# Clustered attention and a softplus feed-forward: the first batch prepared by head pairs, split weights for half of the first pass, and matmuls without data in TensorE's waits

## The chip, the cores and the metric

The kernel runs on 1 core of a Trainium2 chip. The metric is the device time of one execution in microseconds (us). A core has TensorE (PE, matmuls and transposes by matmul into PSUM), VectorE (DVE), ScalarE (ACT), GpSimd (POOL) and SyncE (SP, which here issues DMA transposes and stores). Each engine works through its own rows in order; semaphores order them against each other.

## The reference

Attention over 4 batches of 8 heads, 768 tokens, 64 channels, in which a query sees only the keys of its own cluster; then a feed-forward layer with softplus:

```python
q_n = q / (norm(q) + 1e-06); k_n = ...; c_n = ...           # unit vectors
q_assign = argmax(einsum('bhsd,hcd->bhsc', q_n, c_n))       # 16 clusters a head
k_assign = argmax(einsum('bhsd,hcd->bhsc', k_n, c_n))
mask = q_assign[..., :, None] == k_assign[..., None, :]
scores = where(mask, q @ k.T / sqrt(D), -1e9)
attn = exp(scores - max); attn = attn / (sum(attn) + 1e-9)
x = (attn @ v)                                              # 3072 tokens x 512
h = x @ w_in                                                # 512 x 2048
out = (max(h, 0) + log1p(exp(-abs(h)))) @ w_out             # 2048 x 512
```

Inputs are float32, the two weight matrices float64. The kernel keeps float32 accuracy with pairs of float16 numbers (a high part and the rest).

## The kernel before, in words

The work goes in eight passes: four batches, each in two halves of the queries. A pass has 24 score tiles (8 heads, 3 tiles of 128 queries each). A tile's steps are: `scores`, four matmuls on TensorE against all 768 keys (L544; the second half of the contraction holds the low parts and 16 columns that carry the mask); the row maximum on VectorE (L560); the exponential on ScalarE (L568); then the attention weights must be turned so that keys lie on partitions. In the first pass this is done in float32: six transposes on TensorE (L585), one half evicted by ScalarE (L593), the other by VectorE (L591), and `attend` multiplies in float32 (L647). In the other passes the weights are split (ScalarE casts the high part, L607, GpSimd subtracts, L609), and two tiles together go through one DMA transpose of 24 blocks, a *flip*, issued by SP (L209); `attend` then takes 18 short float16 matmuls (L651 to L653). After two heads the output is normalised (VectorE L670 to L678), split (L685, L687) and turned by a flip of 6 blocks into `xT`.

Before a batch's scores, `prep_k` (two heads at a time) and `prep_q` (four heads) split the inputs, turn them (on TensorE for batch 0, by flips later) and find each token's cluster: short matmuls against the centroids (L394, L395) and some nine VectorE rows on them. `clusters` marks the clusters that hold a key.

The feed-forward part of a pass is `ffn1` (16 blocks of 12 matmuls, `softplus` behind each) and `ffn2` (two halves, three tiles, 24 matmuls each). It starts when all four `xT` pieces of its pass are there and runs beside the scores of the next pass. `prep_weights` splits the float64 weights in 32 steps of 512 columns: a load, one row on ScalarE, three on VectorE (L305, L309, L315), a cast on ScalarE (L318), a subtraction on GpSimd (L319).

What sets the order: the class `Order` runs all these as coroutines while the program is built. Each step names its engine and a cost; the planner takes the step that can start soonest by these costs, the lower priority number first, and emits its instruction. So each engine's order is fixed at build time. Rings (`ring("h", 2)` and the like) stand for the buffers.

## Time and profile before

| | us |
|---|---|
| median of 3 runs | 906.73 (905.98 to 908.38) |
| profiled execution | 904.0 |
| its span | 902.2 |
| TensorE busy | 823.7 (91%) |
| ScalarE busy | 589.4 (65%) |
| VectorE busy | 560.8 (62%) |
| GpSimd busy | 523.9 (58%) |
| mean granted TensorE clock | 0.973 |

The span runs from the first to the last instruction of the profiled execution. An engine's share is an average over the whole span; the views by stretch of time, which the prediction shows, tell the stages apart. "PEclk" is the clock that TensorE was granted.

### The profile page before, as it was taken

To read this page: it belongs to the slowest core of one execution; us is meant where nothing else is said; L and a number is where in the kernel's file an instruction comes from. 1 tells how busy PE (TensorE), PEld (TensorE's weight loads), DVE (VectorE), ACT (ScalarE), POOL (GpSimd) and SP (SyncE) were. 2 spreads that over 40 slices of the span, in tenths; PEclk is the share of its full clock that TensorE was granted. 3 is DMA by queue.
4 is the path that set the end of the run, shared out by engine and by line. 5 is a ranking of instruction groups with operands and counts; after the bars stand their busy time and mean duration, and the time that the engine had idled before them with its cause. 6 is when DMAs were issued, how large, how long until landed. Compare 5 with 4: busy or idle time off the path is not lost.

```text
span 902.2 us, 19238 instructions
## 1 busy us (share of the span) xinstructions
PE 823.7 (91%) x7843; PEld 520.0 (58%) x7843; DVE 560.8 (62%) x1034; ACT 589.4 (65%) x904; POOL 523.9 (58%) x353
## 2 busy tenths in 40 slices
PE   2669797889679999999999999999999999999996
PEld 2558684555335666666666666666666666655542
DVE  5889787778685665675766666666665645433331
ACT  5657477886458877876767777867677676633320
POOL 5233326896548778777677676776676565512210
PEclk9979699999799999999999999999999999999998
DMA  6323439999546979999888779998867755600000
GB/s 222 95 94 120 130 128 195 199 226 237 141 123 159 202 171 202 223 203 230 157 199 179 162 149 206 207 211 182 171 155 161 133 115 138 126 9 25 12 1 35
DMA packets 393320, 136.02 MB, mean 151 GB/s; under 512 B 369680, under 2 KB 386064, under 8 KB 393232
## 3 DMA queue, kind: packets, MB, share of 16 engines
q1 hardware_dynamic: 371472, 99.15, 54.9%
q10 hardware_dynamic: 21760, 35.66, 13.0%
q8 instruction: 61, 1.00, 0.5%
q14 instruction: 27, 0.22, 0.1%
HBM read 35.68 MB, written 6.29 MB: 47 GB/s over the span
## 4 chain that ended last, share of the span: by engine, by line
PE 72%; DMA 4%; DVE 3%; POOL 3%; issue 2%; ACT 2%; POOLq 0%; DVEq 0%; ACTq 0%
PE s L544 10%; PE o L786 9%; PE o L784 9%; PE o L785 9%; PE h L720 8%; PE h L722 8%; PE h L721 8%; PE av L651 3%; PE av L653 3%; PE av L652 3%; DMA pt<-phl 3%; POOL phl L609 2%; DMA xT<-xn 1%; ACT p L568 1%; DVE negm L560 1%
## 5 line engine op out<-in xcount | busy, mean ns | idle before, releaser
L609 POOL TENSOR_TENSOR phl<-p,phl 128x768 f16<-128x768 f32 x168 | 277.2, 1666 | 90.9 <-ACT phl L607 54.2
L560 DVE TENSOR_REDUCE negm<-s 128x1 f32<-128x768 f32 x192 | 182.9, 954 | 67.5 <-PE s L544 65.2
L568 ACT ACTIVATE p<-s,negm 128x768 f32<-128x768 f32 x192 | 172.3, 898 | 72.9 <-DVE negm L560 47.7
L763 POOL TENSOR_TENSOR gh<-fg,gh 128x768 f16<-128x768 f32 x64 | 105.7, 1652 | 134.5 <-ACT gh L762 134.0
L720 PE MATMUL h<-xT,wi 128*128 128x384 f16 x512 | 167.9, 328 | 14.6 <-DVE fg L751 6.2
L722 PE MATMUL h<-xT,wi 128*128 128x384 f16 x512 | 168.1, 328 | 0.0
L721 PE MATMUL h<-xT,wi 128*128 128x384 f16 x512 | 168.0, 328 | 0.0
L544 PE MATMUL s<-kt,qt 128*128 128x384 f16 x768 | 158.5, 330 | 10.2 <-ACT p L568 10.0
L784 PE MATMUL o<-wo,gh 128*128 128x512 f16 x384 | 146.3, 381 | 4.9 <-ACT gh L762 3.3
L786 PE MATMUL o<-wo,gh 128*128 128x512 f16 x384 | 146.5, 382 | 1.4 <-POOL gh L763 1.4
L785 PE MATMUL o<-wo,gh 128*128 128x512 f16 x384 | 146.4, 381 | 0.1
L741 ACT ACTIVATE fa<-fa 128x384 f32<-128x384 f32 x128 | 66.6, 521 | 114.8 <-DVE fa L739 114.1
L607 ACT CAST phl<-p 128x768 f16<-128x768 f32 x168 | 134.1, 827 | 7.1 <-DMA pt<-phl 5.5
L739 DVE TENSOR_SCALAR fa<-h 128x384 int32<-128x384 int32 x128 | 71.1, 556 | 104.0 <-PE h L722 102.8
L651 PE MATMUL av<-vb,pt 128*128 128x65 f16 x1008 | 108.7, 192 | 1.9 <-DMA pt<-phl 1.8
L652 PE MATMUL av<-vb,pt 128*128 128x64 f16 x1008 | 108.7, 192 | 0.0
L653 PE MATMUL av<-vb,pt 128*128 128x65 f16 x1008 | 108.4, 194 | 0.0
L544 PEld LDWEIGHTS <-qt 128*128 128x128 f16 x768 | 72.7, 99 | 58.5 <-issue 15.1
L751 DVE SCALAR_TENSOR_TENSOR fg<-h,fa 128x384 f32<-128x384 f32 x128 | 70.6, 552 | 57.1 <-ACT fa L742 54.5
L651 PEld LDWEIGHTS <-pt 128*128 128x128 f16 x1008 | 93.6, 98 | 15.7 <-DMA pt<-phl 3.4
L652 PEld LDWEIGHTS <-pt 128*128 128x128 f16 x1008 | 92.9, 97 | 11.8
L653 PEld LDWEIGHTS <-pt 128*128 128x128 f16 x1008 | 93.1, 97 | 0.0
(114 smaller groups left out, 1193.6 us busy)
## 6 DMA issues: line engine op xcount, KB each, us to landing
wo<-in_moe_w_in_dram ACTq DMA_DIRECT2D x16, 512.0 KB, 3.6
wo<-in_moe_w_out_dram ACTq DMA_DIRECT2D x14, 512.0 KB, 3.9
rawk<-in_k_dram ACTq DMA_DIRECT2D x16, 384.0 KB, 4.8
rawv<-in_v_dram ACTq DMA_DIRECT2D x16, 384.0 KB, 4.8
rawq<-in_q_dram ACTq DMA_DIRECT2D x16, 384.0 KB, 4.2
out_dram<-ot SPq DMA_DIRECT2D x24, 256.0 KB, 2.5
pt<-phl SPq DMA_TRANSPOSE x84, 5.5
wraw<-in_moe_w_out_dram ACTq DMA_DIRECT2D x2, 512.0 KB, 3.7
```

The costliest lines, as they stand in the source:

```text
L544: nc.tensor.matmul(st[:, j, :SH], qt[:, s, i], kt[:, s, NT // 2 * j : NT // 2 * (j + 1)], start=(s == 0), stop=(s == 1),)
L560: yield op("DVE", 950, lambda: nc.vector.tensor_reduce(negm, st[:, :, :SH], AX.XY, ALU.max, negate=True))
L609: "POOL", 1640, lambda: nc.gpsimd.tensor_tensor(phl[:, u, 1], p32, phl[:, u, 0], ALU.subtract), shared=True
L651: nc.tensor.matmul(av, pt[:, 0, c], vb[:, c, D : 2 * D + 1], start=(c == 0), stop=False)
L652: nc.tensor.matmul(av[:, :D], pt[:, 0, c], vb[:, c, :D], start=False, stop=False)
L653: nc.tensor.matmul(av, pt[:, 1, c], vb[:, c, D : 2 * D + 1], start=False, stop=(c == NT - 1))
L720: nc.tensor.matmul(hp, w[0], x[0], start=(c == 0), stop=False)
L721: nc.tensor.matmul(hp, w[0], x[1], start=False, stop=False)
L722: nc.tensor.matmul(hp, w[1], x[0], start=False, stop=(c == NP - 1))
L784: nc.tensor.matmul(po, g[0], wo[:, f, 0, 0], start=(f == f0), stop=False)
L785: nc.tensor.matmul(po, g[0], wo[:, f, 0, 1], start=False, stop=False)
L786: nc.tensor.matmul(po, g[1], wo[:, f, 0, 0], start=False, stop=(f == f0 + NF // 2 - 1))
```

## The change

The planner and the start of the program change; the arithmetic of each step stays, except where it says so.

- **Head pairs.** Batch 0's Q is prepared two heads at a time (`first_q`), a score tile waits for its own two heads, K's two layouts share one buffer, and the low-part copy on ScalarE goes for batch 0. Early results may use whichever PSUM bank is free (`bank`); evictions go to the engine that the planner finds free (`evict`).
- **Split weights from tile 12 on.** `MIX` has one letter for two tiles: the first six pairs of the first pass stay float32, the other six take the split path with flips.
- **Fill-ins.** Before a TensorE step with a planned wait over 600 ns, `warm` emits matmuls of 120 columns on constants into an unused part of the attention bank, as many as fill 65% of the wait at 52 ns each: 1251 in the program.
- **Weight steps in pace.** Step s waits for score tile 1.4 s.
- **The last `xT` piece** of the first pass is turned by TensorE; the planner's DMA model has separate clocks for loads and flips, and a subtraction or cast may be given to VectorE at a penalty of 2000 ns, which the new order never does.

```diff
+WGATE = 0
+WPACE = 1.4
+WARM = 120
+WARM_FROM = 600
+WARM_SHARE = 0.65
+MIX = "ffffffhhhhhh"
+EARLY = "hos"
+PTB = "ho"
...
             self.active.remove(ch)
-            _, eng, ns, emit, opt = ch["op"]
+            if eng == "PE" and self.warm:
+                self.warm(start - self.free["PE"])
...
+    mbank = ps_m.tile([P, 512], F32, name="mbank")
+    idle = mbank[:, 512 - WARM :]
+
+    def warm(gap):
+
+        if gap > WARM_FROM:
+            for _ in range(int(gap * WARM_SHARE / 52)):
+                nc.tensor.matmul(idle, eye, ones[:, :WARM], start=True, stop=True)
...
+    def evict(dst, src, size):
+
+        return op(
+            ("ACT", "DVE"),
+            (180 + size * 0.8, 160 + size * 1.04),
+            (lambda: nc.scalar.copy(dst, src), lambda: nc.vector.tensor_copy(dst, src)),
+        )
+
+    def sub(dst, a, b, size):
+
+        return op(
+            ("POOL", "DVE"),
+            (150 + size * 1.95, 120 + size * 1.08),
+            [lambda e=e: e.tensor_tensor(dst, a, b, ALU.subtract) for e in (nc.gpsimd, nc.vector)],
+            shared=True,
+            bias=BIAS,
+        )
+
+    banks = {"s": (ps_s, 2), "h": (ps_h, 2), "o": (ps_o, 1)}
+
+    def bank(tags, shape, dtype, name):
+
+        tag = next((t for t in tags if od.room(t, banks[t][1])), tags[0])
+        key = yield from ring(tag, banks[tag][1])
+        return key, banks[tag][0].tile(shape, dtype, tag=tag, name=name)
...
-        yield op("ACT", 630, lambda: nc.scalar.activation(mag, val, AF.Abs, scale=sc))
+        gate = int(WGATE + step * WPACE)
+        if gate >= 0:
+            yield wait("sc", gate)
+        yield op("ACT", 660, lambda: nc.scalar.activation(mag, val, AF.Abs, scale=sc))
...
-        yield op("ACT", 830, lambda: nc.scalar.copy(n2[:, :, :D], n1[:, :, D:]))
-        od.set(nk)
+        if n >= H:
+            k2, n2 = yield from next_n2()
+            keys.append(k2)
+            yield op("ACT", 830, lambda: nc.scalar.copy(n2[:, :, :D], n1[:, :, D:]))
...
+    def first_q(n: int):
+
+        qkey[n, 0] = yield from ring("qt", 2)
+        nt = passes[0][2]
+        rk, qf = yield from load_q(n, 0)
+        qt = p2.tile([P, 2, 4, nt, P], F16, tag="qt", name=f"qt_{n}_0")
+        for u in range(4):
+            qT[n + u, 0] = qt[:, :, u]
+        for u in (0, 2):
+            od.spawn(prep_q(n + u, 0, 2, qf[:, u : u + 2], qt[:, :, u : u + 2], rk if u else None), od.cur["prio"] + u * nt)
...
+    def whole(t):
+
+        return t < H * QT and MIX[t // 2] == "f"
...
-        yield wait("q", n - n % 4, pi)
+        yield wait("q", n - n % (4 if pi else 2), pi)
...
-        if pi == 0:
+        if whole(t):
...
-        yield flip(
-            xT[pi][:, pr].rearrange("p s c t -> p (s c) t"), t_.rearrange("p s c d -> p (s c d)"), 2 * QT
+        yield from turn(
+            xT[pi][:, pr].rearrange("p s c t -> p (s c) t"),
+            t_.rearrange("p s c d -> p (s c) d"),
+            f"xT_{pr}_{pi}",
+            pi == 0 and pr == NP - 1,
         )
...
-        od.spawn(prep_weights(step), begin - 12 + step * 0.6)
+        od.spawn(prep_weights(step), WGATE + WDUE + step * WPACE)
```

Three places show how the order moves. The first is VectorE at its first two row maxima (`negm`); before, the rows ahead of them end the Q preparation of heads 0 to 7:

```order
L506 TENSOR_TENSOR sim_q_0_539<-sim_q_0_539,al_292 128x192
L499 TENSOR_SCALAR n_1_114<-sim_q_0_549 128x12x16
L511 TENSOR_REDUCE aq_0_617<-sim_q_0_539 128x12
L506 TENSOR_TENSOR sim_q_0_549<-sim_q_0_549,al_463 128x192
L511 TENSOR_REDUCE aq_0_621<-sim_q_0_549 128x12
L309 SCALAR_TENSOR_TENSOR wo<-wo,wi 128x512
L305 TENSOR_SCALAR wi<-wi 128x512
L380 COPY qt_0_374<-qT_0_0_6_635 128x768
L380 COPY qt_0_412<-qT_4_0_6_651 128x768
L560 TENSOR_REDUCE negm_0_667<-s_0_654 128x1
L560 TENSOR_REDUCE negm_1_672<-s_1_666 128x1
```

Now:

```order
L608 TENSOR_TENSOR sim_q_0_319<-sim_q_0_319,al_427 128x96
L475 TENSOR_REDUCE best_k_592<-sim_k_504 128x12
L613 TENSOR_REDUCE aq_0_613<-sim_q_0_319 128x6
L514 TENSOR_TENSOR sim_k_504<-sim_k_504,best_k_592 128x192
L671 TENSOR_REDUCE negm_0_611<-s_0_590 128x1
L516 TENSOR_SCALAR kn_4_152<-sim_k_504 128x12x16
L251 COPY qt_0_141<-qT_2_0_0_620 128x384
L582 SCALAR_TENSOR_TENSOR qn_4_0_506<-rawq_0_131,qn_4_0_506 128x6x64
L533 TENSOR_REDUCE sim_k_504<-sim_k_504 128x32
L251 COPY qt_0_141<-qT_2_0_3_655 128x384
L535 TENSOR_SCALAR al_663<-sim_k_504 128x32
L671 TENSOR_REDUCE negm_1_675<-s_1_652 128x1
```

The first maximum is row 67 instead of row 100 of VectorE, and the preparation of heads 4 to 7 now stands between the maxima; the weight rows (L305, L309) stand behind them.

The second place is ScalarE's start, from the centroids' norm (`cnrm`) to the first casts of K (`kn`). Before:

```order
L227 ACTIVATE cnrm<-csg 128x1
L228 ACTIVATE cnrm<-cnrm 128x1
L423 CAST kn_0_136<-rawk_124 128x12x64
L351 CAST vb_104<-rawv_125 128x12x64
L253 COPY cents<-centsT 128x384
L204 DMA rawq_141<-in_q_dram 128x4x192
```

Now:

```order
L297 ACTIVATE cnrm<-cnrm 128x1
L273 DMA rawv_134<-in_v_dram 128x2x384
L322 COPY cents<-centsT 128x384
L499 CAST kn_0_137<-rawk_125 128x12x64
L578 ACTIVATE qn_0_0_142<-rawq_0_126 128x6x64
L578 ACTIVATE qn_2_0_143<-rawq_0_126 128x6x64
```

The first cast of K stood ahead of the copy of the turned centroids and stands behind it, with the first two Q casts beside it.

The third place is SP's start; `pt` are the attention weights of two tiles, `qt` is Q of the next pass, `xT` attention output. Before:

```order
L209 DMA_TRANSPOSE xT_928<-xn_0_916 128x6x128
L209 DMA_TRANSPOSE qt_1_994<-qn_0_1_995 128x12x128
L209 DMA_TRANSPOSE xT_928<-xn_0_1138 128x6x128
L209 DMA_TRANSPOSE qt_1_994<-n_0_112 128x12x128
L209 DMA_TRANSPOSE xT_928<-xn_0_1362 128x6x128
L209 DMA_TRANSPOSE qt_1_1423<-qn_4_1_1424 128x12x128
L209 DMA_TRANSPOSE pt_4_1528<-phl_3_1458 128x24x128
L209 DMA_TRANSPOSE xT_928<-xn_0_1517 128x6x128
```

Now:

```order
L278 DMA_TRANSPOSE xT_1135<-xn_0_1115 128x6x128
L278 DMA_TRANSPOSE qt_1_1191<-qn_0_1_1192 128x12x128
L278 DMA_TRANSPOSE pt_1_1301<-phl_0_1234 128x24x128
L278 DMA_TRANSPOSE pt_0_1383<-phl_2_1282 128x24x128
L278 DMA_TRANSPOSE xT_1135<-xn_0_1352 128x6x128
L278 DMA_TRANSPOSE qt_1_1191<-n_0_112 128x12x128
L278 DMA_TRANSPOSE pt_2_1542<-phl_1_1386 128x24x128
L278 DMA_TRANSPOSE pt_1_1695<-phl_0_1430 128x24x128
L278 DMA_TRANSPOSE xT_1135<-xn_0_1858 128x6x128
L278 DMA_TRANSPOSE pt_0_1906<-phl_2_1652 128x24x128
L278 DMA_TRANSPOSE pt_2_1995<-phl_1_1706 128x24x128
```

Six flips of 24 blocks now belong to the first pass, and its fourth `xT` flip is gone.

350 lines of the change are left out of this document (193 added, 157 removed).

## The prediction

> **What bounds the kernel now.** I read the page's slices first, then the busy time in eight stretches, which I cut where the maxima of score tiles 0, 12, 24, 45, 48 and 57 end on VectorE (row max L560, one per tile), then where TensorE's last ffn1 matmul ends.
>
> ```profile
> span 902.2 us, 19238 instructions
> PE   2669797889679999999999999999999999999996
> PEclk9979699999799999999999999999999999999998
> ```
>
> The columns of the next view: stretch, its length, busy us (and instructions) of TensorE, weight loads, VectorE, ScalarE, GpSimd, then granted clock, DMA share, GB/s.
>
> ```profile
> 0.00:56.50 56.50, 25.32 (x303) 20.46 (x303) 40.14 (x117) 28.60 (x41) 22.64 (x23) 0.91 0.44 145
> 56.50:88.60 32.10, 29.23 (x236) 25.42 (x237) 31.39 (x50) 25.30 (x52) 10.32 (x9) 1.00 0.37 110
> 88.60:133.20 44.60, 38.68 (x277) 32.60 (x275) 36.51 (x63) 26.64 (x54) 12.61 (x11) 0.81 0.42 125
> 133.20:197.70 64.50, 52.39 (x592) 35.12 (x591) 48.19 (x80) 53.39 (x80) 51.00 (x34) 1.00 0.98 199
> 197.70:254.70 57.00, 45.79 (x434) 26.77 (x433) 40.72 (x77) 31.43 (x52) 33.75 (x23) 0.88 0.88 203
> 254.70:284.40 29.70, 24.54 (x186) 13.87 (x185) 22.45 (x38) 23.02 (x35) 20.54 (x13) 1.00 0.41 108
> 284.40:877.80 593.40, 592.81 (x5772) 360.14 (x5770) 338.26 (x610) 399.17 (x591) 371.43 (x240) 1.00 0.73 152
> 877.80:902.20 24.40, 14.97 (x56) 5.63 (x54) 3.19 (x5) 1.88 (x3) 1.64 (x1) 0.86 0.09 32
> ```
>
> The reader is to see two programs. From 284.4 to 877.8 TensorE is busy 592.81 of 593.40 us: nothing but fewer matmul columns can shorten that. Before 284.4 it is not the bound. In the first two stretches VectorE is (31.39 of 32.10 us in the second); then no engine is full, and chains between ScalarE, VectorE, GpSimd and the flips (DMA transposes, 0.98 and 0.88 of the DMA engines) set the pace. So TensorE work removed there is worth nothing by itself; an earlier tile 57 is worth its whole gain. I call the six early stretches A to F.
>
> **The method.** The changed program's order shows which rows stand between the same tiles. I priced them with the means of the groups below (VectorE's copy of a half tile, the weight split on each engine, ScalarE's casts), and took 0.935 of the sum, because neighbouring instructions overlap: the same count of the old order then gives VectorE 32.9, 38.7, 47.6 us in B, C, D against 31.39, 36.51, 48.19 above.
>
> ```profile
> L609 POOL TENSOR_TENSOR phl<-p,phl 128x768 f16<-128x768 f32 x168 | 277.2, 1666 | 90.9 <-ACT phl L607 54.2
> L560 DVE TENSOR_REDUCE negm<-s 128x1 f32<-128x768 f32 x192 | 182.9, 954 | 67.5 <-PE s L544 65.2
> L607 ACT CAST phl<-p 128x768 f16<-128x768 f32 x168 | 134.1, 827 | 7.1 <-DMA pt<-phl 5.5
> L591 DVE COPY ptf<-pT 128x384 f32<-128x384 f32 x24 | 13.2, 550 | 3.3 <-PE pT L585 3.2
> L318 ACT CAST wi<-wo 128x512 f16<-128x512 f32 x16 | 10.4, 659 | 6.9 <-DVE wo L315 6.7
> L303 ACT ACTIVATE wi<-wo 128x512 f32<-128x512 f32 x16 | 10.8, 678 | 6.1 <-DMA wo<-in_moe_w_in_dram 6.1
> L315 DVE SCALAR_TENSOR_TENSOR wo<-wo 128x512 int32<-128x512 int32 x30 | 26.6, 886 | 0.2
> L309 DVE SCALAR_TENSOR_TENSOR wo<-wo,wi 128x512 int32<-128x512 int32 x16 | 12.4, 775 | 0.3
> L305 DVE TENSOR_SCALAR wi<-wi 128x512 int32<-128x512 int32 x16 | 10.0, 626 | 0.1
> ```
>
> **A, to tile 0: 56.5 becomes 36 us.** The new order has two thirds as many rows on VectorE ahead of the first maximum (67 for 100), worth 23.4 us for the old 40.14: two heads' K and Q instead of all eight, and no weight work. One thing goes the other way. ScalarE's first K cast moves from ahead of the centroids' copy to behind it.
>
> ```profile
> 6.59 0.81 ACT L423 CAST kn<-rawk 128x768 f16<-128x768 f32 x1
> 6.92 0.22 DVE L231 SCALAR_TENSOR_TENSOR cnrm<-crn,csg,cnrm 128x1 f32<-128x1 f32 x1
> 7.56 1.59 DVE L231 SCALAR_TENSOR_TENSOR cnrm<-crn,csg,cnrm 128x1 f32<-128x1 f32 x1
> 11.31 0.58 PE L250 MATMUL centsT<-eye,cb 128*128 128x128 f16 x3 [11.31 <-DVE cb L242]
> 11.68 1.57 PE L376 MATMUL kT<-eye,kn 128*128 128x128 f16 x12
> 11.93 0.48 ACT L253 COPY cents<-centsT 128x384 f16<-128x384 f16 x1 [3.79 <-PE centsT L250]
> ```
>
> L231 takes 0.22 us alone and 1.59 beside GpSimd's K subtraction. With that subtraction later it shortens by 1.4, so the centroids' copy ends near 11 instead of 12.4; the cast (0.8) and the subtraction (1.6) follow, and K's transposes start near 13.4 instead of 11.7. After their eviction VectorE has, from about 16.5, another 16 us of rows, and I add 3 for its waits on TensorE and GpSimd: 36. Bounds: 32 with no wait; 40 with the 16.4 us that VectorE idles in A now.
>
> **B, tiles 0 to 11: 32.1 becomes 42.** The remaining heads' K and Q land here: 41.3 us on VectorE, which stays the bound. Bounds 41 and 46.
>
> **C, tiles 12 to 23: 44.6 becomes 34.** These tiles now use split weights. TensorE loses 12 times float32 work, priced here (starts of neighbours):
>
> ```profile
> 66.49 1.45 PE L647 MATMUL av<-rawv,ptf 128*128 128x64 f32 x12
> 67.77 0.50 PE L585 MATMUL pT<-eye,p 128*128 128x128 f32 x3
> 68.11 0.81 PE L544 MATMUL s<-kt,qt 128*128 128x384 f16 x4
> 68.76 1.45 PE L647 MATMUL av<-rawv,ptf 128*128 128x64 f32 x12
> 147.49 0.19 PE L651 MATMUL av<-vb,pt 128*128 128x65 f16 x1
> 148.58 0.32 PE L720 MATMUL h<-xT,wi 128*128 128x384 f16 x1
> ```
>
> That is 1.28 + 2 x 0.34 = 1.96 us a tile, against 1.09 us for two tiles of split weights: 17 us of TensorE in all, off the bound. What counts is VectorE (26.9 us for 38.7), against GpSimd, which gets 12 subtractions of 1666 ns (30.5 us busy), and ScalarE 28.8. Six flips of 24 blocks go to SP's queue here; they pass no work they delay, since DMA is at 0.42. With GpSimd at 90%: 34. Bounds 31 and 41 (the ratio of C now, 44.6 to 36.51, on VectorE's 26.9 gives 33; two buffers for split tiles in flight may give more).
>
> **D, tiles 24 to 44: 64.5 becomes 76.** The pacing of the weight steps puts 13 of them here instead of 5: 8 more, each 2.3 us of VectorE and 1.3 of ScalarE. Busy becomes 67.9 VectorE, 68.8 ScalarE, 63.6 GpSimd. At the old 83% of the fullest engine it is 83; at 95%, 72. I take 90%, nearer the low end: D no longer holds the start-up of the flips, and the last attention output of the first pass is turned by TensorE (6 transposes and two half copies), so that this wait goes:
>
> ```profile
> PE h L720 <- DMA xT<-xn: 2.9, 1, 2.9
> ```
>
> The loads of the 8 steps (512 KB each) come through the same DMA engines as the flips, at 0.98 in D now; that is the reason for the upper bound.
>
> **E, to tile 48: 57 becomes 46; F, to tile 57: 29.7 becomes 28.** E loses weight and feed-forward rows (VectorE 31.7 us, ScalarE 23.7), and two ffn1 blocks fewer stand ahead of tile 48. The new matter is TensorE's fill-ins, matmuls of 120 columns without data, 1251 of them in its order. The nearest row is the score matmul: four of 384 columns in 0.65 us, so 51 ns for 120. 86 are in the tail, 17 far behind, 1148 ahead of tile 57: 59 us at full clock. They stand in planned waits, 65% of each. Counted with them TensorE has 43 us in E and 26 in F, which sets 46 and 28. Bounds 43 to 53, and 27 to 31. Six fill-ins must also wait until VectorE has read the attention bank; a score tile stands behind them, VectorE's three rows take 0.9 us, and I count 2 us, in D.
>
> The six sum to 262 us for 284.4, so 22 us.
>
> **Behind tile 57.** The row of 593.40 holds, but in the new order ffn1 stands 3.5 blocks back at that tile. A block is 12 matmuls of 384 columns, 1.95 us: +6.8. The order at the end is the same but for the fill-ins.
>
> **The tail.**
>
> ```profile
> 877.76 0.33 PE L722 MATMUL h<-xT,wi 128*128 128x384 f16 x1
> 881.38 0.39 PE L784 MATMUL o<-wo,gh 128*128 128x512 f16 x1 [3.29 <-ACT gh L762]
> 883.49 0.63 PE L784 MATMUL o<-wo,gh 128*128 128x512 f16 x1
> 883.92 0.63 PE L785 MATMUL o<-wo,gh 128*128 128x512 f16 x1
> 896.67 0.38 PE L785 MATMUL o<-wo,gh 128*128 128x512 f16 x1
> 896.89 0.38 PE L786 MATMUL o<-wo,gh 128*128 128x512 f16 x1
> ```
>
> After the wait of 3.29 us thirteen matmuls are 0.43 apart instead of 0.215. The 64 fill-ins take 3.3 us, as long as the wait, and keep the clock: -2.8. Bounds 0 and -2.8.
>
> **The clock, row and rule.** 94.6 to 111.6 is a stretch at about half clock:
>
> ```profile
> 94.60:111.60 17.00, 12.48 (x76) 10.66 (x77) 12.28 (x25) 8.02 (x17) 4.65 (x4) 0.56 0.41 119
> ```
>
> TensorE was busy 73% of it and stayed slow for 17 us, so fill-ins over 65% of the waits need not keep the clock up: if they do not, the first rival's time follows. [...]
>
> **The sum.** 262 + 593.4 + 6.8 + (24.4 - 2.8) = 883.8 us of span for 902.2. The profiled execution took 904.0, 1.8 more than its span; the median of the runs shown is 906.73, so I add 4.5 to the span: **888 us**, 2.1% faster.
>
> **Rivals.**
> *The fill-ins meet a half clock* (slower). Place: TensorE from tile 12 to 57. By the order it has 120 us of real work there at full clock and 50 of fill-ins, 170 in C to F, for which I forecast 184. At half clock every 10% of that adds 17 us. It uses up the 14 us of room at 8%, and the gain of 18.4 at 19%. With 30% (clocks of 0.81 over 44.6 and 0.88 over 57 us mean 31 us at half in 102 now) it is 170 + 51 = 221 for 184: 925 us. For it speaks the row of 12.48 in 17 us; against it, that the fill-ins stand in the waits. Chance 0.08.
> *The weight steps fill D, and its neighbours stay loose* (no change). With C, D, E and F at their upper bounds, tile 57 comes at 36 + 42 + 41 + 83 + 53 + 31 = 286 us, later than now, and the run at 286 + 600.2 + 21.6 + 4.5 = 912; with half of these misses at 900. For it: in D three engines and the DMA stand within 10% of each other, so a row that is placed badly on one costs all. Against: C's long time now is in part half clock. Chance 0.12, for 900 to 912, half of it below 904.
> *The early stage is only as long as its fullest engine.* A 33, B 41, C 32, D 72, E 43, F 27 sum to 248: 248 + 600.2 + 21.6 + 4.5 = 874. For it: half clock in C and E (0.81 and 0.88) and the single Q chain for four heads are gone. Against: no stretch but B reaches it now. Chance 0.25.
>
> **How the numbers follow.** My case 0.55, the low one 0.25, no change to slightly slower 0.12, slower 0.08. The range runs from 867 (the low case without ffn1's lag of 6.8) to 906. About 0.3% (904 to 909.5) is what a measurement tells from no change. Faster: 0.55 + 0.25 + 0.06 = 0.86; of the other 0.06, 0.05 within 0.3%; slower 0.01 + 0.08 = 0.09.
>
> **What would show it.** Right: the first L671 ends near 36 us and tile 12's near 78, with VectorE above 95% busy between; tile 24's near 112; tile 45's gains almost nothing over 197.7 (188); tile 57's near 262; TensorE full from there; the last matmuls 0.215 apart. Wrong: fill-ins 100 ns apart beyond tile 12, or TensorE's waits behind fill-ins on VectorE over a few us; a clock below 0.95 in C or E; or a TensorE with waits beyond tile 57, which would mean that the lag in ffn1 or the added flips reach the steady part.

## The result, and the profile after

The changed kernel takes **921.12 us** (median of 4 runs, 919.29 to 922.72) against 907.41 us for the kernel before in the same comparison: ratio 1.0162, interval 1.0135 to 1.0189. It is 1.6% slower; I had forecast 888 us and faster. The profiled execution took 921.07 us, 1.8 more than its span. Medians, here and in the table of runs, are over all executions of a kernel, while ratios and intervals leave out three slow ones (one each of after_src_on, all_f32_phl_off and all_f32_slow_weights).

From the page of the changed kernel, the span and the slices of TensorE, its clock and the DMA:

```profile
span 919.3 us, 21779 instructions
PE   7998769899699999999999999998999999999997
PEclk7999999999899999999999999999999999999999
DMA  6338898989869799999996899989978766620000
```

The busy times of the changed kernel by stretch, cut as in the prediction (maxima L671 of tiles 0, 12, 24, 45, 48, 57, then the last ffn1 matmul, L838; columns as there):

```profile
0.00:31.00 31.00, 23.51 (x343) 21.98 (x343) 18.77 (x84) 16.99 (x27) 18.84 (x23) 0.83 0.57 196
31.00:70.20 39.20, 37.26 (x393) 32.84 (x391) 36.09 (x78) 32.95 (x67) 9.53 (x9) 1.00 0.38 117
70.20:104.60 34.40, 28.13 (x426) 24.08 (x426) 24.63 (x43) 23.34 (x33) 21.41 (x15) 1.00 0.98 192
104.60:200.40 95.80, 80.30 (x1145) 61.16 (x1143) 72.37 (x113) 70.56 (x106) 72.84 (x50) 0.98 0.89 192
200.40:252.10 51.70, 43.82 (x545) 30.00 (x544) 31.97 (x63) 24.65 (x40) 31.77 (x22) 0.95 0.97 182
252.10:281.60 29.50, 28.28 (x291) 18.80 (x290) 21.29 (x38) 22.05 (x32) 15.36 (x10) 0.97 0.69 150
281.60:897.30 615.70, 604.29 (x5834) 365.28 (x5833) 342.62 (x619) 400.84 (x599) 375.64 (x243) 1.00 0.78 147
897.30:919.30 22.00, 16.74 (x140) 9.51 (x137) 3.19 (x5) 1.88 (x3) 1.64 (x1) 1.00 0.10 37
```

The reader is to see three things. The start works: tile 24 is reached at 104.6 us, 28.6 earlier than before, at a clock of 1.00 from tile 0 on. Stage D then takes 95.8 us instead of 64.5 and eats all of it. And behind tile 57 TensorE is no longer full: 604.29 busy of 615.70 us, 11.4 us of waits where there were 0.6, at the same clock of 1.00.

What TensorE waits for there (the view of waits of TensorE, 281 to 897 us, changed kernel; total, times, longest):

```profile
PE mbank L758 <- DMA pt<-phl: 9.4, 9, 3.1
PE sim_q L466 <- DMA qt<-qn: 1.5, 1, 1.5
```

These are flips. The DMA view has their duration, first of the kernel before (queue q1 carries the flips; the last number of the other row is the median from issue to landing):

```profile
q1 hardware_dynamic: 371472, 99.15, 54.9%
pt<-phl SPq DMA_TRANSPOSE x84, 5.5
```

and of the changed kernel:

```profile
q1 hardware_dynamic: 389296, 103.67, 63.3%
pt<-phl SPq DMA_TRANSPOSE x90, 6.8
```

4.6% more bytes take 17% more time of the DMA engines (63.3% of 919.3 against 54.9% of 902.2 us), and a flip of the same 24 blocks takes 6.8 us instead of 5.5. It is so in the steady part too, 6.6 for 5.4 between 300 and 780 us, where the DMA moves 170 GB/s for 177.

The trace keeps every DMA packet. I gave the 256 B packets of q1, less the 128 of the load of the centroids at the start, to the flips in order of issue; then a flip's own transfer can be read, from its first packet to its last, and the share of its packets that took over 20 ns (most take 18). Beside it stands where the source buffer begins in SBUF, from the built program. All of it behind 300 us:

```
kernel          flip           source, bytes past      first to last   packets
                               a multiple of 256       packet, us      over 20 ns
before          phl, 24 blocks       0                   3.00             1.4%
before          qn1, 12 blocks     128                   2.01            12.7%
before          n2 (q), 12 blocks    0                   1.52             0.6%
changed         phl, 24 blocks     128                   3.86            15.7%
```

The change had moved phl. Buffers are laid out in the order in which they are first asked for; in the new program the keys kn12 of the first batch use phl's buffers, so that these come right behind n1, 128 B past a multiple of 256 B, where n1 lies in both kernels. No line of the diff names an address.

### The profile page after: what moved, and what is told of

The parts are those of the page before. It is cut to its first block, busy times and chain, and to the rows that moved or that the text cites. A ratio compares the mean times of both kernels' runs of the same rounds, so it can differ in the third digit from the quotient of the medians.

```text
span 919.3 us, 21779 instructions
## 1 busy us (share of the span) xinstructions
PE 862.3 (94%) x9100; PEld 563.7 (61%) x9100; DVE 550.9 (60%) x1036; ACT 593.3 (65%) x904; POOL 547.0 (60%) x371
## 3 DMA queue, kind: packets, MB, share of 16 engines
q1 hardware_dynamic: 389296, 103.67, 63.3%
## 4 chain that ended last, share of the span: by engine, by line
PE 57%; DMA 13%; DVE 5%; POOL 5%; issue 4%; ACT 3%; POOLq 0%; ACTq 0%; DVEq 0%
DMA pt<-phl 11%; PE s L655 8%; PE o L902 7%; PE o L904 7%; PE o L903 7%; PE h L836 6%; PE h L838 6%; PE h L837 6%; POOL phl L259 3%; PE mbank L758 3%; PE mbank L760 2%; PE mbank L759 2%; DVE negm L671 1%; ACT phl L715 1%; DMA qt<-n 1%
## 5 line engine op out<-in xcount | busy, mean ns | idle before, releaser
L259 POOL TENSOR_TENSOR phl<-p,phl 128x768 f16<-128x768 f32 x180 | 297.2, 1666 | 91.9 <-ACT phl L715 64.1
L671 DVE TENSOR_REDUCE negm<-s 128x1 f32<-128x768 f32 x192 | 182.9, 954 | 81.6 <-PE s L655 79.1
L655 PE MATMUL s<-kt,qt 128*128 128x384 f16 x768 | 157.8, 329 | 14.7 <-ACT p L679 9.3
L838 PE MATMUL h<-xT,wi 128*128 128x384 f16 x512 | 167.1, 326 | 0.0
L715 ACT CAST phl<-p 128x768 f16<-128x768 f32 x180 | 143.7, 828 | 25.7 <-DMA pt<-phl 23.4
L758 PE MATMUL mbank<-vb,pt 128*128 128x65 f16 x1080 | 117.1, 193 | 14.6 <-DMA pt<-phl 14.6
L758 PEld LDWEIGHTS <-pt 128*128 128x128 f16 x1080 | 100.6, 98 | 33.0 <-DMA pt<-phl 20.4
L759 PE MATMUL mbank<-vb,pt 128*128 128x64 f16 x1080 | 117.0, 193 | 0.0
L760 PE MATMUL mbank<-vb,pt 128*128 128x65 f16 x1080 | 116.7, 195 | 0.0
L759 PEld LDWEIGHTS <-pt 128*128 128x128 f16 x1080 | 100.2, 97 | 11.6 <-issue 0.3
L760 PEld LDWEIGHTS <-pt 128*128 128x128 f16 x1080 | 100.4, 97 | 0.0
```

Source lines behind the costliest of these rows:

```text
L259: [lambda e=e: e.tensor_tensor(dst, a, b, ALU.subtract) for e in (nc.gpsimd, nc.vector)],
L655: nc.tensor.matmul(st[:, j, :SH], qt[:, s, i], kt[:, s, NT // 2 * j : NT // 2 * (j + 1)], start=(s == 0), stop=(s == 1),)
L671: yield op("DVE", 950, lambda: nc.vector.tensor_reduce(negm, st[:, :, :SH], AX.XY, ALU.max, negate=True))
L758: nc.tensor.matmul(av, pt[:, 0, c], vb[:, c, D : 2 * D + 1], start=(c == 0), stop=False)
L759: nc.tensor.matmul(av[:, :D], pt[:, 0, c], vb[:, c, :D], start=False, stop=False)
L760: nc.tensor.matmul(av, pt[:, 1, c], vb[:, c, D : 2 * D + 1], start=False, stop=(c == NT - 1))
```

## The experiments

All runs, with the ratio to the kernel before on the same chip. "phl on" means that phl begins on a multiple of 256 B.

```
run                    phl  first pass  other edit              us      ratio and interval
the change             off  half split                          921.12  1.0162  1.0135 to 1.0189
before_phl_off         off  (before)                            915.19  1.0083  1.0057 to 1.0109
after_phl_on           on   half split                          914.30  1.0066  1.0026 to 1.0106
after_src_on           on   half split  n1 on, too              908.65  1.0006  0.9975 to 1.0037
all_f32_phl_off        off  float32                             912.95  1.0058  1.0021 to 1.0094
all_f32                on   float32     n1 on                   893.99  0.9868  0.9843 to 0.9894
all_f32_pt_on          on   float32     n1 on, pt on            895.20  0.9841  0.9788 to 0.9894
phl_on_no_fill         on   half split  no fill-ins             916.23  1.0104  1.0072 to 1.0137
all_f32_no_fill        on   float32     n1 on, no fill-ins      905.95  0.9975  0.9947 to 1.0002
last_two_split         on   4 split     n1 on                   907.28  1.0012  0.9975 to 1.0049
half_flips             on   half split  n1 on, six half flips   904.02  0.9986  0.9954 to 1.0018
half_flips_short_sub   on   half split  and six short subs      906.32  1.0011  0.9992 to 1.0031
sub_shared             on   half split  n1 on, BIAS 300         917.12  1.0125  1.0092 to 1.0157
all_f32_sub_shared     on   float32     n1 on, BIAS 300         916.83  1.0115  1.0066 to 1.0164
late_weights           on   half split  n1 on, w_out later      950.38  1.0494  1.0469 to 1.0519
f32_weights_early      on   float32     n1 on, old due times    922.97  1.0201  1.0172 to 1.0231
weights_faster         on   half split  n1 on, WPACE 0.9        906.72  1.0015  0.9988 to 1.0041
all_f32_slow_weights   on   float32     n1 on, WPACE 1.9        905.00  0.9982  0.9953 to 1.0010
all_f32_fast_weights   on   float32     n1 on, WPACE 0.9        896.57  0.9890  0.9844 to 0.9935
```

Where the time lies, by the ends of the maxima of score tiles in the profiled executions (us):

```
tiles        before  change  after_src_on  half_flips  late_weights  all_f32
0 to 12        32.1    39.2      39.3         39.3        39.3         39.3
12 to 24       44.6    34.4      35.4         34.8        35.5         39.8
24 to 36       32.6    58.3      56.0         54.8        51.3         35.3
36 to 45       31.9    37.5      36.4         36.4        30.7         42.0
45 to 57       86.7    81.2      75.4         73.8        43.1         54.4
57 to 191     497.1   519.1     512.2        512.8       599.8        530.2
```

### Placement

The edit is an unused buffer ahead of a named one; it shifts what is laid out behind it and changes no instruction's place.

```
+    pads = {"phl": 32}
+    on_p2 = lambda shape, dtype, tag, **kw: (tag in pads and p2.tile([P, pads.pop(tag)], F32,
+        tag="pad" + tag, name="pad" + tag, bufs=1), p2.tile(shape, dtype, tag=tag, **kw))[1]
...
-            pair[t // 2] = p2.tile([P, 2, 2, 2, SH], F16, tag="phl", name=f"phl_{sfx}"), key
+            pair[t // 2] = on_p2([P, 2, 2, 2, SH], F16, tag="phl", name=f"phl_{sfx}"), key
```

(every p2.tile becomes on_p2; 32 words of float32 are 128 B). before_phl_off puts this into the kernel before; after_phl_on has {"phl": 32, "fa": 32} in the changed kernel, after_src_on {"n1": 32, "fa": 32}.

> The kernel before, with one unused buffer of 128 B per partition put into SBUF ahead of phl, so that phl begins 128 B past a multiple of 256 B, where it lies in the changed kernel (before: on a multiple of 256 B). Nothing else is moved but fg behind it, which no flip reads; the order of every engine is the same. Theory 1 (placement): the flips of phl read rows that straddle a 256 B line. The median from issue to landing goes from 5.5 us to between 6.5 and 7, the share of queue q1 from 54.9% to 62 or 63, TensorE beyond tile 57 is no longer 99.9% busy, and the time rises by 10 to 25 us, to 917 to 932. Rival (order and load): the flips got slower in the changed kernel because there are six more of them, because they stand closer together and because loads run beside them. Then this kernel runs like the one before, 907 within 3 us, with 5.5 us a flip.

> The changed kernel, with one unused buffer of 128 B ahead of phl and one behind it, so that phl begins on a multiple of 256 B as it does in the kernel before and all that follows moves by 256 B. The order of every engine is the same. Theory 1 (placement): a flip of phl takes 5.5 us again, q1 falls from 63.3% to about 57, TensorE beyond tile 57 is 99% busy or more, the stretch from tile 57 to 191 shrinks from 519 to about 499 us, and stage D, which was fed by flips, by 5 to 10 us. Time 888 to 900. Rival (order and load): 921 within 3 us, flips still at 6.5 us or more.

> As after_phl_on, but the first buffer of 128 B stands ahead of n1, so that n1 (the source of the first flips of keys and queries, 128 B past a multiple of 256 B in both kernels) and phl both begin on multiples of 256 B: every flip then reads rows on 256 B lines. Theory 1: the flips kt<-kn and qt<-qn, 4.7 to 5.1 us, come down to those of n2, 3.7 to 4.7 us, phl's are as in after_phl_on, and the time is that of after_phl_on or up to 5 us less (26 flips of 168 or so, mostly in the steady part where TensorE hides them). Rival (order and load): 921 within 3 us.

The DMA view of before_phl_off:

```profile
q1 hardware_dynamic: 371472, 99.15, 59.7%
pt<-phl SPq DMA_TRANSPOSE x84, 6.5
```

and of after_phl_on:

```profile
q1 hardware_dynamic: 389296, 103.67, 58.5%
pt<-phl SPq DMA_TRANSPOSE x90, 6.1
```

The same 371,472 packets and the same bytes take 59.7% instead of 54.9% once 128 B stand ahead of phl, and its own transfers go from 3.00 to 3.84 us (16.1% of the packets over 20 ns); on the multiple they are back at 3.02 us in the changed kernel. From issue to landing these take 6.1 us, though, not the 5.5 that I expected: the placement accounts for the transfer itself, not for all of the delay. The steady part answers. One and the same window, 281 to 870 us, of the kernel before and of before_phl_off (columns as above):

```profile
281.00:870.00 589.00, 588.41 (x5748) 357.90 (x5747) 337.46 (x607) 399.00 (x590) 371.96 (x241) 1.00 0.74 154
```

```profile
281.00:870.00 589.00, 584.59 (x5752) 355.39 (x5751) 339.68 (x607) 401.91 (x593) 376.92 (x244) 1.00 0.82 156
```

and of the changed kernel and after_src_on:

```profile
281.00:870.00 589.00, 577.60 (x5690) 351.38 (x5689) 334.29 (x605) 392.62 (x584) 370.73 (x240) 1.00 0.81 154
```

```profile
281.00:870.00 589.00, 582.48 (x5664) 353.15 (x5662) 334.73 (x606) 390.56 (x586) 367.67 (x238) 1.00 0.73 151
```

So the placement is one cause, in both kernels: +0.8% in the kernel before (just under the 10 us that I expected as the least), and in the changed one 1.0% back by moving phl. The profiled executions of before and before_phl_off are 12.2 us apart, 4.5 of them ahead of tile 24, where no flip of phl has run: the clock is granted at 0.75 instead of 0.81 in C there, so the medians, 8.2 us apart, are the better measure. The rival, order and load alone, is out. But my expectation of 888 to 900 was wrong too, and of TensorE busy for 99% or more behind tile 57: after_src_on only draws level with the kernel before, and its TensorE still waits 6.5 of these 589 us, for 0.6 in the kernel before. What causes the other 5.9 us stays open.

That moving n1 helps besides is not shown. The ratios of after_phl_on and after_src_on, 1.0066 and 1.0006, overlap in their intervals, and the flips out of n1's buffers did not get quicker from issue to landing as I had expected (3.7 to 4.7 us): qt<-qn takes 4.8 and kt<-kn 5.6 us, for 4.8 and 5.4 in after_phl_on.

all_f32_pt_on tells that it is the reads that count. It moves the destination, pt, from 64 B past a multiple of 128 B to a multiple of 256 B ({"n1": 32, "pt": 16, "rs": 48, "fa": 32}).

> all_f32 with pt, which the flips of phl write, moved from 64 B past a multiple of 128 B to a multiple of 256 B; sources stay on multiples of 256 B. Theory (the destination counts as well as the source): a flip of phl, 3.0 us from its first packet to its last in the steady part, takes 10% less or more, and the time falls by 1 to 6 us below 894. Rival (only the reads count): 3.0 us a flip, 894 within 2 us.

2.99 us from first packet to last against 3.00 in all_f32, and the same time within the intervals: the rival holds, for this one pair of destinations.

### Float32 weights for the whole first pass

```
-MIX = "ffffffhhhhhh"
+MIX = "ffffffffffff"
```

all_f32 is after_src_on with this line; all_f32_phl_off is the changed kernel with this line and nothing else.

> As after_src_on, but all 24 tiles of the first pass use float32 weights (MIX is twelve f), so that the six flips of tiles 12 to 23 are gone. What is open: tiles 24 to 45 take 92 us in after_src_on (105.8 to 198.2), 64.5 in the kernel before, 76 by my forecast, and TensorE has 41 of 60 us with nothing real to do between 80 and 140. Theory F (split tiles in stage C): a split tile goes through ScalarE, GpSimd and a flip, with two buffers for it, and tiles 12 to 23 use these up before tile 24, so that D has no start from empty buffers any more and begins with a DMA that is full. Then tiles 24 to 45 come down to 65 to 72 us here, tiles 12 to 24 take 42 to 46 instead of 35, tile 57 comes at 260 to 266 instead of 273.6, and the time is 895 to 905. Theory W (weight steps in stage D): the pacing puts 14 weight steps between tiles 24 and 45, and GpSimd and ScalarE stand behind their chains. Here it still puts 10 there: tiles 24 to 45 stay at 80 us or more, and with the slower stage C the time is 908 to 920.

> The changed kernel with float32 weights for all of the first pass and nothing else: phl stays where the change put it, 128 B past a multiple of 256 B (with all_f32 it makes a pair that differs in placement alone, with the changed kernel a pair that differs in the split tiles alone). Theory (two causes that add): it takes what all_f32 takes, 894, plus what the placement cost with the split tiles, 921.1 less 908.7: 904 to 909. Rival (the placement counts only where the six additional flips fill the DMA): 894 to 898.

all_f32 is the best kernel of this study, 1.3% faster than the one before, though its TensorE has 12 tiles of float32 work more to do than after_src_on. Its stretches C, D and E:

```profile
69.50:109.30 39.80, 36.30 (x355) 32.93 (x355) 33.43 (x62) 27.85 (x57) 12.69 (x12) 1.00 0.46 115
109.30:186.60 77.30, 68.17 (x824) 49.19 (x823) 67.52 (x102) 61.78 (x96) 58.40 (x39) 1.00 0.93 196
186.60:219.10 32.50, 32.50 (x366) 20.33 (x363) 22.89 (x47) 22.11 (x35) 27.32 (x19) 1.00 1.14 236
```

D is 77.3 us, for 92.4 in after_src_on: between theory F, which said 65 to 72, and theory W, which said 80 or more. Tile 57, at 241.0 us, and the time, 893.99, are better than either said. C lost only 4.4 us by the float32 work. Tile 57 comes 32.6 us earlier, but only 14.7 of these reach the end: the order behind it differs, and 30 more ffn1 matmuls, 30 more of ffn2 and 137 more fill-ins stand behind tile 57 (4.9, 6.5 and about 7 us by the spacings of 0.162, 0.215 and 0.051 us). With phl off, the one line still brings 921 to 913, ratios 1.0162 and 1.0058 without overlap; that is 4 us above what I expected, and far from the rival's 894 to 898. Within the intervals the two causes add: the placement of phl and n1 together costs 1.6% with split tiles and 1.9% without, the split tiles 1.0% with phl off and 1.4% with phl on.

Is the cost per flip? last_two_split splits four tiles only.

```
+MIX = "ffffffffffhh"
```

> all_f32 with split weights for the last four tiles of the first pass (two additional flips instead of six). Theory F in its plain form (each additional flip costs the same, 908.7 less 894.0 over six, 2.4 us): 899. Rival (the first two pairs go into empty buffers at no cost, as at the start of stage D in the kernel before, and spare 7.8 us of float32 work on TensorE): 890 to 894.

Four split tiles cost as much as twelve, 907.28 against 908.65. Both of my cases are wrong: it is no price per flip, and it is not free. The tiles tell why. In every kernel the first eight split tiles run at 2.0 to 3.6 us each, into empty buffers, and the twelve behind them more slowly, at 3.5 to 4.8 us a tile: in last_two_split tile 27 ends at 110.5 us and tile 33 at 141.3, in the changed kernel tile 24 at 104.6 and tile 36 at 162.9, in the kernel before tiles 24 to 36 take 2.7 us each and 36 to 45 3.5. A float32 tile takes 3.3 us (39.8 us for twelve). As I read it, the change does not remove a slow start of the split tiles; it moves their quick start 12 tiles ahead and runs their slow rate through stage D. That empty buffers make the start quick is argued from these rates; no run changes the buffers alone.

What sets this slow rate? Two runs take work away from the flips and from GpSimd's subtractions of tiles 12 to 23; the order of every engine stays, and the odd tiles read the even tile's weights:

```
         yield flip(
-            pt.rearrange("p u s c t -> p (u s c) t"), phl.rearrange("p u s j t -> p (u s j t)"), 4 * NT
+            pt[:, : 1 + (t >= H * QT)].rearrange("p u s c t -> p (u s c) t"),
+            phl[:, : 1 + (t >= H * QT)].rearrange("p u s j t -> p (u s j t)"), 4 * NT
...
-            pts[t - 1 + w] = pt[:, w], ptk
+            pts[t - 1 + w] = pt[:, w if t >= H * QT else 0], ptk
```

and, for half_flips_short_sub, besides:

```
-        yield sub(phl[:, u, 1], p32, phl[:, u, 0], S)
+        w = 32 if u and t < H * QT else SH
+        yield sub(phl[:, u, 1, :, :w], p32[:, :, :w], phl[:, u, 0, :, :w], S)
```

> after_src_on with the order of every engine unchanged, but the six flips of tiles 12 to 23 carry only the even tile of each pair (12 blocks instead of 24), and the attention of the odd tiles reads the even tile's result: the outputs of six tiles of each core's first pass are not computed. Theory DMA (the DMA is busy 0.93 and more from tile 12 to 48, and the six flips' time adds to it): 1.5 us less for each flip, and with the loads beside them as much as 2: tile 57 comes 9 to 12 us earlier than 273.6 and the time falls by 5 to 12 us. Theory chain (SP waits 44 of the 60 us between 85 and 145 for what it is to flip; the flips are short beside that): tile 57 within 4 us, the time within 4 us of after_src_on's 908.7.

> half_flips, and of GpSimd's subtractions for the odd tiles 13 to 23, whose result nothing reads then, only 64 of 768 columns are done: six times about 1.5 us of GpSimd less. Theory chain with GpSimd as its slowest part: tile 24 and tile 45 come 5 to 9 us earlier than in half_flips. Theory DMA, or a chain that GpSimd does not set: within 2 us of half_flips.

half_flips brings tile 57 3.6 us earlier and the time to 904, whose interval overlaps that of after_src_on; the work taken away from GpSimd on top brings nothing (tile 45 at 198.3 for 196.2). So neither the DMA time of the six added flips nor GpSimd's subtractions for their odd tiles hold stage D up. Both runs leave the flips and subtractions of tiles 24 to 45 whole. For D's own flips after_phl_on is a weak test: between 100 and 200 us, with loads beside them, their transfers take 4.0 us for 4.2 in the change, and D is 95.6 us for 95.8. For GpSimd's work on D's own tiles no run with the same order is a test. Both stay open. The queue that issues flips stood waiting most of the time, not moving data: in after_src_on, 85 to 145 us, the waits of SP's DMA queue are

```profile
SPq L278 <- POOL wi L259: 16.6, 4, 6.5
SPq L278 <- POOL phl L259: 13.9, 4, 6.7
SPq L278 <- POOL n L618: 7.2, 1, 7.2
SPq L278 <- POOL xn L259: 6.6, 1, 6.6
```

44 of 60 us, each wait ended by a row of GpSimd, so that GpSimd stays a candidate. Giving a third of the subtractions to VectorE (BIAS 300 instead of 2000) changes the order as well, and is worse with and without split tiles in the first pass:

> after_src_on with the planner's handicap of 2000 ns for subtractions on VectorE lowered to 300 ns: VectorE takes 59 or so of the 180 subtractions of split tiles in the whole program. Theory chain with GpSimd as its slowest part: tiles 24 to 45 fall from 92 to 80 us or less, and the time by 5 to 12 us. Theory DMA: tiles 24 to 45 stay within 4 us of 92.

> all_f32 with the handicap lowered in the same way (47 subtractions of split tiles go to VectorE). Theory chain with GpSimd: stage D, 77 us, shrinks by 5 or more and the time falls to 885 to 890. Theory DMA: D stays and the time is 894 within 3 us. A third possibility is that VectorE, which would run the subtractions between maxima, becomes the longer wait in the steady part: then 896 or more.

917.12 and 916.83: tiles 24 to 45 are 93.6 and 83.5 us, for 92.4 and 77.3, although GpSimd is busy only 25.1 and 25.5 us of them; VectorE is busy 81.5 and 76.3. The lower handicap also moves work in stage A, where tile 0 now ends near 37 us instead of 31.

### The weight steps in stage D

The waits of all engines of the changed kernel between 70 and 200 us name them (five of the eleven rows; the longest, VectorE's 15.9 us for the scores, is that of a tile for TensorE):

```profile
POOL wi L259 <- ACT wi L393: 11.1, 6, 3.1
POOL wo L259 <- ACT wo L393: 9.7, 5, 2.9
ACT wi L393 <- DVE wo L387: 9.2, 6, 2.1
POOL phl L259 <- ACT phl L715: 7.7, 5, 3.1
ACT p L679 <- POOL phl L259: 7.4, 8, 1.5
```

GpSimd stands 20.8 us before subtractions of weights whose cast ScalarE has not done, and ScalarE stands 9.2 us in front of that cast for VectorE. The tiles' own rows are behind each of these. So I moved the steps.

```
-        gate = int(WGATE + step * WPACE)
+        gate = int(WGATE + step * WPACE) + (24 if step > 16 else 0)
...
-        od.spawn(prep_weights(step), WGATE + WDUE + step * WPACE)
+        od.spawn(prep_weights(step), WGATE + WDUE + step * WPACE + (24 if step > 16 else 0))
```

> As after_src_on, but weight steps 17 to 31 (w_out) are due 24 score tiles later: of the 14 weight steps between tiles 24 and 45 seven are left, all before tile 34. Theory W: tiles 33 to 45, 55.8 us in after_src_on, fall to 42 or less (3.5 us a tile, the rate of the kernel before between tiles 36 and 45), while tiles 24 to 33 stay at 36 us. Theory F: tiles 33 to 45 stay within 4 us of 55.8. The time says little, since the second feed-forward matmuls of the first pass must wait for w_out: I expect 905 to 930.

Two windows of late_weights, tiles 24 to 33 and 33 to 45:

```profile
105.50:141.00 35.50, 26.92 (x501) 23.27 (x499) 25.57 (x37) 22.55 (x31) 26.83 (x19) 1.00 0.80 181
141.00:187.50 46.50, 43.90 (x588) 32.01 (x586) 31.83 (x64) 37.34 (x58) 34.85 (x24) 1.00 1.09 210
```

46.5 us for 55.8: between the two theories, which said 42 and 52. Seven steps fewer are worth 9.3 us there at most, since the second feed-forward matmuls are missing from this stretch too. The whole run loses 42 us, more than I expected, because these matmuls then wait for w_out. The other paces:

```
f32_weights_early       -        od.spawn(prep_weights(step), WGATE + WDUE + step * WPACE)
(with MIX all f)        +        od.spawn(prep_weights(step), begin[0] - 12 + step * 0.6)
                        -WGATE = 0
                        +WGATE = -1000
weights_faster          -WPACE = 1.4
all_f32_fast_weights    +WPACE = 0.9
all_f32_slow_weights    +WPACE = 1.9
```

> As all_f32, with the weight steps due as in the kernel before (from the tenth tile ahead of the first feed-forward block, 0.6 tiles apart, with no gate) instead of one in 1.4 score tiles. The changed planner then places 8 steps ahead of tile 24 (17 in the kernel before) and 14 behind tile 45. Theory F: like all_f32, 895 to 905, and tiles 24 to 45 at 65 to 72 us. Theory W: tiles 24 to 45 are shorter than in all_f32 by 3 us for each weight step less, and the time goes with them.

> As after_src_on, with a weight step in 0.9 score tiles instead of 1.4. By its order 15 steps stand ahead of tile 24 instead of 10, 9 to 10 between tiles 24 and 45 instead of 14, and all 32 are done by tile 48. Theory W: tiles 24 to 45 shrink by 10 us or more, tiles 12 to 24 grow by 5, and the time falls by 5 to 10 us below after_src_on. Theory F: tiles 24 to 45 stay within 5 us of 92, and the time is within 5 us of after_src_on.

> all_f32 with a weight step in 1.9 score tiles instead of 1.4: 5 steps stand between tiles 24 and 45 instead of 10. Theory (each weight step there holds the rows of the tiles back by 1.3 us, as late_weights showed: 9.3 us for seven): tiles 24 to 45 take 71 instead of 77 us; the second half of the weights comes later, so that the time is within 6 us of 894 on either side. Rival (the rows of the weight steps fit into the waits): 77 us within 2.

> all_f32 with a weight step in 0.9 score tiles: 16 steps ahead of tile 24 instead of 15, 9 between tiles 24 and 45 instead of 10. Theory (weight steps): 76 us there and 894 within 3 us. Rival (the planner's whole order changes, and the time with it): anything up to 10 us above 894 with no change of the steps' number to account for it.

The old due times are the worst with float32 tiles: tile 0 ends at 39.9 us instead of 30.2, and the time is 923. With WPACE 0.9 and split tiles, stage D does not shrink (90.8 us for 92.4), against theory W. With 1.9 and float32 tiles, D is 73.9 us for 77.3 with five steps fewer: 0.7 us a step, half of what I expected, and the 11 us lost in the whole run are elsewhere, later in the weights' wake. With 0.9 and float32 tiles D is 76.9 us and the time 896.57, as the first theory said. By these runs a weight step costs D 0.3 to 1.3 us; the nine that D has more than in the kernel before are worth 3 to 12 of the 31 us by which it grew, not all of them. What sets the 4 to 5 us of a split tile in stage D beyond that stays open; what is left is the order itself, in which each of three engines waits for the next with rows of tiles, weights and the next batch's heads between.

### The fill-ins

```
-    od.warm = warm
+    od.warm = None
```

> As after_phl_on, without the fill-in matmuls (they write a part of a bank that nothing reads; the output is the same). Theory A (my step in stage D: the fill-ins that wait for VectorE's reading of the bank cost about 2 us): the time is that of after_phl_on less 0 to 3 us if TensorE's clock stays granted without them. Theory B (the fill-ins hold the clock, as meant): stages A to F show granted clocks of 0.8 to 0.9 as the kernel before did (0.81 in C, 0.88 in E), each such dip costs the TensorE work in it 10 to 20%, and the time is 3 to 12 us above after_phl_on.

> all_f32 without the fill-in matmuls. Theory B (they hold the clock): all_f32 ran at a mean granted clock of 0.998 with TensorE waiting 45 us between 100 and 280; without them the granted clock falls below 0.9 in the stretches with waits and the time is 3 to 12 us above 894. Theory A (they delay the work behind them and the clock would hold): 894 or up to 3 us less.

With split tiles the two medians, 916.23 and 914.30, do not separate, although the clock does fall without fill-ins, to 0.81, 0.80 and 0.83 in C, D and E. D of phl_on_no_fill:

```profile
106.80:199.60 92.80, 67.16 (x675) 42.60 (x675) 69.17 (x113) 70.39 (x106) 72.80 (x50) 0.80 0.89 194
```

That is no longer than the 95.6 us of after_phl_on at a clock of 0.96: the granted clock is not what sets D there. In the all-float32 kernel the fill-ins are worth 12 us, 0.9975 against 0.9868. C and D of all_f32_no_fill:

```profile
72.20:116.80 44.60, 40.36 (x294) 35.62 (x294) 34.02 (x62) 28.08 (x57) 12.68 (x12) 0.81 0.38 104
116.80:196.80 80.00, 62.65 (x587) 40.15 (x586) 69.72 (x102) 61.70 (x96) 58.93 (x40) 0.89 0.88 195
```

The granted clock is 0.81 and 0.89, where all_f32 has 1.00 in both with the same real work, and C takes 44.6 us for 39.8. Fill-ins over 65% of the waits do not always hold it: in after_phl_on, which has them, C is at 0.90.

A TensorE row of all_f32_no_fill and a window behind it show the fall of the clock in C:

```profile
81.32 0.20 PE L466 MATMUL sim_q<-cents,qt 128*128 128x16 f16 x1 [2.35 <-DMA qt<-qn]
81.30:97.50 16.20, 16.05 (x90) 13.82 (x90) 8.60 (x19) 6.88 (x15) 3.50 (x3) 0.50 0.38 102
```

The wait of 2.35 us is TensorE's longest in C, and the clock stays at half for 16 us in which TensorE is busy 99%. How long a wait must be to bring the half clock, and what ends it, no run here isolates.

## Why the prediction was wrong

By its own steps, forecast against the profiled run (us):

```
step          forecast   measured   with phl and n1 on
A                36        31.0        31.1
B                42        39.2        39.3
C                34        34.4        35.4
D                76        95.8        92.4
E                46        51.7        47.9
F                28        29.5        27.5
behind tile 57  600.2     615.7       608.7
tail             21.6      22.0        22.0
span            883.8     919.3       904.3
```

**A and B: the mechanism right, the sums too large.** VectorE's rows ahead of tile 0 cost 18.8 us, not 23.4; in B it is the bound, as said, 36.09 of 39.2 us, where 41.3 were counted. Both stretches are shorter than my lower bounds of 32 and 41, together 7.8 us of further gain.

**C: the length right by luck, the sentences under it wrong.** "With GpSimd at 90%: 34." GpSimd was busy 21.41 of the 34.4 us, 62%, and not the 30.5 that I had put there: a tile's row maximum comes before its weights are split, so only eight of the twelve subtractions fell into C. The rest of its work came in D. "Six flips of 24 blocks go to SP's queue here; they pass no work they delay, since DMA is at 0.42." The 0.42 belonged to a stage without flips: it is 0.98 now. The price of split tiles in C is paid in D.

**D: the step that failed.** "I take 90%, nearer the low end: D no longer holds the start-up of the flips." D took 95.8 us, 19.8 more than this, of the 35.5 by which the span missed. Two terms were wrong. The work was: GpSimd had 72.84 us to do in D, not 63.6, which at 90% makes 81 us. And the share was: the fullest of the three engines was busy 76%, not 90%, and less than the old 83%. The sign of the argument for 90% is wrong. The start-up of the split tiles is their quick part: 2.7 us a tile between tiles 24 and 36 of the kernel before, whose row of 64.5 us for D therefore already had it. Pricing D by the fullest engine's busy share could not see it; the rate in two parts of the stage could. Tiles 24 to 33 and 33 to 45 of the kernel before, of the change and of all_f32:

```profile
133.20:156.40 23.20, 16.77 (x162) 11.78 (x161) 17.00 (x30) 17.19 (x25) 13.41 (x9) 1.00 0.93 193
156.40:197.70 41.30, 35.63 (x432) 23.34 (x431) 31.19 (x52) 36.20 (x56) 37.59 (x25) 1.00 1.00 202
```

```profile
104.60:143.50 38.90, 28.23 (x501) 24.17 (x499) 24.39 (x37) 23.79 (x34) 26.84 (x20) 0.96 0.77 172
143.50:200.40 56.90, 52.06 (x648) 36.99 (x646) 47.98 (x78) 46.77 (x73) 46.01 (x31) 1.00 0.98 205
```

```profile
109.30:132.00 22.70, 19.27 (x236) 14.92 (x234) 20.36 (x33) 17.86 (x26) 15.83 (x11) 1.00 0.78 175
132.00:186.60 54.60, 48.90 (x588) 34.27 (x589) 47.15 (x71) 43.93 (x70) 42.57 (x29) 1.00 0.99 205
```

The first part grew by 15.7 us, and with float32 tiles in C it is as quick as before (22.7 us in all_f32, 36.6 in after_src_on): this half of the growth comes with the split tiles of C. Whether it is their backlog or the weight work that moved with it (six subtractions of weights for two in all_f32) no run separates. The second part grew by 15.6 us, and with float32 tiles it is nearly as slow: this half has another cause. The weight steps have a share in it, since late_weights takes 46.5 us there without seven of them and without second feed-forward matmuls, and 44 more ffn1 matmuls, 7 us by their spacing, stand in it than before. That D of all_f32, 77.3 us, comes out near my 76 does not bear the sum out: the work in it is 58.40 us of GpSimd and 61.78 of ScalarE, for 63.6 and 68.8. The placement of phl shows no part in D (95.8 and 95.6 us with phl off and on).

**E and F: right once phl is in place**, 45.9 and 27.5 us in after_phl_on, together 7.8 us less than with phl off, with TensorE busy 43.3 and 26.6 us, as counted (43 and 26).

**Behind tile 57: the mechanism of the lag right, its stretch not full.** 42 more ffn1 matmuls stand behind tile 57, 3.5 blocks, 6.8 us as forecast. The other 15.5 us are 10.8 more of waits, nearly all for flips, and 4.7 of other and slower work (626 to 630 us ran at a granted clock of 0.57). "The row of 593.40 holds" is the sentence that failed here, and the prediction took for granted that a flip keeps its 5.5 us. The placement is not all of it: with phl and n1 on their multiples the stretch is 608.7 us, still 8.5 above the forecast, and why is open. No edit in the diff names phl's address; it was to be had from the built program, and a hint of the price is in the trace of before: its flips of qn1, 128 B off, take 2.01 us for 12 blocks, those of n2, on the multiple, 1.52. It is a hint only, since few of these flips stand behind 300 us and their times scatter: on the multiple, in after_src_on, qn1's packets over 20 ns fall to 2.3%, but nine flips still have a median of about 2.07 us. For the 24 blocks of phl the runs of one order give 3.84 us off the multiple for 3.00 on it in the kernel before, and 3.86 for 3.02 in the changed one, 1.28 times in both; how the placement comes to cost this, no run shows.

**The tail**: 2.4 us shorter for the 2.8 forecast. The -2.8 in the sum, and E and F at full clock, rest on fill-ins that keep the clock, which no run had shown when I forecast it; the changed kernel then had a granted clock of 1.00 in the tail, for 0.86 before, 0.95 in E and 0.97 in F.

**The rivals.** The half clock did not come to stay (0.95 to 1.00 in the stretches from tile 12 on), and fill-ins, which I charged with 2 us, waited 4.1 us for VectorE in three places:

```profile
  DVE x L792: 4.1, 3
```

(the changed kernel's view of the instructions on mbank, 80 to 281 us), but in the float32 version they return more than they cost; with split tiles it is not shown. "The weight steps fill D, and its neighbours stay loose" came nearest, with tile 57 at 286 us and 912 as its end, though not by its cause alone: C was tight, E and F came near its 53 and 31 us, D went past its 83, and the weight steps account for a part of that only. Its end lacks the 15.5 us behind tile 57. No rival had the slower flips; the slower side held 0.09, which was far too little for a change that moves every buffer and the order of every engine.

**Among the signs** I had named the right one: "a TensorE with waits beyond tile 57, which would mean that the lag in ffn1 or the added flips reach the steady part". It came, in part by neither: the placement accounts for some of the waits, and the rest stays open.

## What to carry to other kernels

When a change adds, removes or first uses a buffer elsewhere, compare the addresses of all DMA transposes' sources in the two built programs: 128 B past a multiple of 256 B made the transfer of a 24-block flip 28% longer here (3.84 us for 3.00) and the run 7 to 8 us by phl alone, 12 to 19 with n1, with no line of the diff to show it, and an unused buffer of 128 B gives it back. Read the rate of a stage in parts before pricing a change that moves work into it: the first split tiles were quick only once, and moving them earlier moved the slow rate as well. Ask also whether the mark that ends a stage, here a row maximum, comes before the work that the stage is priced by: what is left over is paid in the next. Parts of one change can have opposite signs: the start by head pairs (tile 12 at 70.2 us for 88.6) and, with float32 tiles, the fill-ins gain, the split weights and the placement lose, and without the losers the same change is 1.3% faster than the kernel before.

## What the runs showed of the hardware that was not expected

The transfer of the 24-block DMA transposes of phl out of SBUF depended on where the source begins: 3.00 to 3.02 us on a multiple of 256 B (1 to 2% of the 256 B packets over 20 ns), 3.84 to 3.86 us at 128 B past one (16%), in two programs each. Moving the destination from 64 B past a multiple of 128 B to a multiple of 256 B made no difference (3.00 us in all_f32, 2.99 in all_f32_pt_on). Matmuls without data in the waits raised the clock: in all_f32 they keep TensorE busy 88% to 100% of C to E at a granted clock of 1.00; without them it was 0.81 and 0.89 in C and D, and the run 12 us longer. In all_f32_no_fill a wait of 2.35 us was followed by 16.2 us at a granted clock of 0.50, with matmuls for 16.05 of them. And the order matters at the scale of these effects: moving the weights' due times or a third of one kind of subtraction, with the same work, spread the float32 versions over 894 to 923 us.
